# Delta-rule attention in front of two MLPs: state and solved rows as block-diagonal tiles, more fillers at the head of TensorE's queue, weight conversion in three passes

## The chip, the core and the metric

The kernel runs on one core of a Trainium2 chip. The metric is the device time of one execution in microseconds (us), the lower the better. Several executions are timed, and the median counts. One further execution was profiled: the times of single instructions below come from that one.

The engines are TensorE (PE; PEld is its weight load, which runs beside PE), VectorE (DVE), ScalarE (ACT), GpSimd (POOL) and SyncE (SP, which here only issues DMAs). Each works through its own queue in the order in which the program filled it.

## The reference

Three layers follow each other. First comes an attention with a state that is corrected at each position (the delta rule), 4 batches x 8 heads, 768 positions, 48 values per head:

```python
k_n = k / (np.linalg.norm(k, axis=-1, keepdims=True) + 1e-06)
for t in range(S):
    y[:, :, t] = einsum('bhd,bhde->bhe', q[:, :, t], state)
    v_old = einsum('bhde,bhd->bhe', state, k_n[:, :, t])
    state += beta[t] * einsum('bhd,bhe->bhde', k_n[:, :, t], v[:, :, t] - v_old)
```

Its output, 3072 tokens x 384, goes through two MLPs of width 2048: `g(x @ w_in) @ w_out` with a rational function g, and then the same with `h * tanh(softplus(h))`. The weights reach the core as 64-bit floats; the kernel makes two 32-bit parts of each (high and low), and every MLP product is three products of such parts.

## The kernel before

**Stages.** The attention comes first, on all engines at once, together with the conversion of the first MLP's weights. The two MLPs follow, 192 units of 9 up and 9 down products each; the second MLP's weights are converted beside the first MLP.

**Attention.** The 768 positions are cut into 12 blocks `u` of 64. A tile holds 16 pairs of heads, one head of a pair on the partitions 0 to 63, the other on 64 to 127. For each block there are three pieces of work:

- `prepare(u)`: load k and q (SP), square and sum k (ACT L315, DVE L319), invert the norm for two blocks at a time (DVE L329 to L344, ACT L333), scale k (L396, DVE for the first two blocks, POOL for the others), transpose k and q on PE (L352), copy them out of PSUM (ACT L356), multiply k with k and q (`gram`, PE L367), mask the result (DVE L376), copy blocks (ACT L414).
- `inverse(u)`, once for two blocks: invert a triangular 32 x 32 matrix for each head by 30 dependent steps (L451 and L457), between two 32 x 32 transposes on DVE (L439 `first`, L464 `last`, which writes `xt`) and two scalings by beta (L442, L461). `ON_DVE` puts the ones of blocks 1 and 9 on DVE; those of blocks 3, 5, 7 and 11 run on POOL.
- `step(u)`, in two halves `h`: keys with the state (`ks`, PE L511), subtract from v (`rest`, DVE L519), solve the upper 32 rows (`uu`, PE L528), copy out (`u_out`, ACT L535), `cross` (PE L543), `rest`, `uu` for the lower rows, `u_out`; then the new state (`s_mm`, PE L551; `s_out`, ACT L559) and the output (`y_mm`, two parts for each half, PE L566; `y_out`, ACT L575). Every product here is 64 x 64 or 32 x 32. Two products of different heads lie on opposite corners of the array.

A block can only be prepared when the block six before it is through its step (rings of `NT = 6`), a step needs the `xt` of its pair of blocks, and the state runs from step to step.

**Order.** All attention and conversion work is put into a `Plan` with a cost in ns for each piece. `Plan.best` plays 800 random priority changes through these costs with a greedy list order, keeps the best, and writes the engines' queues in that order. `HOP` is the cost of a handover between engines. Where the plan sees TensorE idle, `run` puts fillers (`heat`, L1060: products with a zero tile) into PE's queue, and 16 of them stand ahead of everything. They read `zero`, which POOL fills at the end of its setup (L1056), and `ident`.

**Conversion.** For each of 32 halves of w1: DMA, `mag` (ACT L669), `size` (DVE, two instructions, L674 and L678), `sign` (DVE L684), `low` (DVE L690), `out` (ACT L697), `rest` (POOL L702), and a DMA back to memory for each whole tile.

**Start of the MLP.** `fetch_x` loads the first rows of the attention's output, `x_hi` (ACT L802) and `x_lo` (POOL L806) split them into the tile `x`.

## Time and profile before

| | us |
|---|---|
| median of 3 runs | 1112.09 (1107.67 to 1112.23) |
| the profiled execution, its own time | 1106.31 |
| its span, first to last instruction | 1104.6 |
| PE busy in the span | 1052.0 (95%) |
| DVE, ACT, POOL busy | 722.8, 605.3, 545.7 |

The busy share of PE says little about the attention: fillers count as busy there, and pipelined products overlap. In the MLPs, from 310 us on, PE streams without a gap. The page's line of the granted clock shows full speed (9 in tenths) nearly throughout, with slices at 8 in the attention. The groups below are cut from the page's views for single stretches; an instruction's row has its start, its length, the engine, the line, what it writes and reads, its shape and how many follow each other as one row, and in brackets how long the engine had been idle and what ended that.

### The profile page before, as it was taken

Reading aid. Unit: us, or ns where it says so; the run is one execution under the profiler, and the core shown is the slowest. Engines: PE = TensorE matmul, PEld = TensorE weight load, DVE = VectorE, ACT = ScalarE, POOL = GpSimd, SP = SyncE. Lnnn points to the kernel's source line nnn. Section 1 sums busy time; section 2 is a strip of 40 time slices with the busy share of each in tenths; the row PEclk is TensorE's granted clock in tenths of the full one; section 3 lists DMA queues with packets and bytes.
Section 4 is the critical chain, followed back from the end, with each engine's and each line's share of the span. In section 5 each row is a group of like instructions: output and inputs, shape, how many; then the busy total and the mean of one; then the engine's idle time right before and its main releaser. Section 6 shows DMA issues by size and latency. Waiting matters only on the chain.

```text
span 1104.6 us, 24807 instructions
## 1 busy us (share of the span) xinstructions
PE 1052.0 (95%) x10128; PEld 898.2 (81%) x10128; DVE 722.8 (65%) x1221; ACT 605.3 (55%) x1081; POOL 545.7 (49%) x623
## 2 busy tenths in 40 slices
PE   5998999888899999999999999999999999999998
PEld 4887888777878878888888888888888888888897
DVE  5997574997669999999999999993222212222211
ACT  3515455433479888988989898743232322223222
POOL 3288797575458778787877878773000000000000
PEclk9999899998999999999999999999999999999999
DMA  6617776425775021121203036250110202011010
GB/s 127 150 30 182 184 202 161 130 61 156 221 263 223 15 101 44 53 76 63 96 10 106 15 127 252 74 177 1 24 34 13 46 1 57 1 23 35 10 20 30
DMA packets 152947, 99.25 MB, mean 90 GB/s; under 512 B 114048, under 2 KB 136192, under 8 KB 152832
## 3 DMA queue, kind: packets, MB, share of 16 engines
q1 hardware_dynamic: 150976, 96.77, 30.4%
q8 instruction: 79, 1.29, 0.5%
q10 hardware_dynamic: 1600, 0.79, 0.3%
q14 instruction: 36, 0.29, 0.1%
q0 software_dynamic: 256, 0.10, 0.1%
HBM read 66.16 MB, written 31.46 MB: 88 GB/s over the span
## 4 chain that ended last, share of the span: by engine, by line
PE 71%; DVE 15%; issue 3%; ACT 3%; DMA 3%; POOL 2%; SPq 2%; DVEq 0%; ACTq 0%; POOLq 0%
PE h L822 31%; PE o L848 28%; PE o L862 3%; PE c_ps L528 2%; PE y_ps L566 2%; DVE tmp L451 2%; PE c_ps L511 1%; SPq L240 1%; PE s_all L551 1%; DVE q L920 1%; DVE r L924 1%; DVE s L911 1%; DVE g L929 1%; DVE xs L457 1%; DMA w<-in_moe_w_in_dram 1%
## 5 line engine op out<-in xcount | busy, mean ns | idle before, releaser
L822 PE MATMUL h<-x,w 128*128 128x512 f32 x1728 | 424.3, 390 | 2.9 <-DVE s L913 2.9
L848 PE MATMUL o<-gh,w 128*128 128x512 f32 x1584 | 387.6, 389 | 0.0
L822 PEld LDWEIGHTS h<-x,w 128*128 128x128 f32 x1728 | 323.3, 188 | 72.3 <-DVE s L913 5.8
L848 PEld LDWEIGHTS o<-gh,w 128*128 128x128 f32 x1584 | 297.3, 188 | 61.8
L837 DVE TENSOR_TENSOR gh<-g,gh 128x512 fp32r<-128x512 f32 x80 | 55.0, 687 | 231.4 <-ACT g L949 231.4
L944 ACT ACTIVATE gh<-h 128x512 fp32r<-128x512 f32 x96 | 57.5, 599 | 261.0 <-PE h L822 261.0
L837 POOL TENSOR_TENSOR gh<-g,gh 128x512 fp32r<-128x512 f32 x112 | 149.5, 1336 | 83.5 <-ACT gh L833 62.0
L897 POOL TENSOR_TENSOR q<-q,r 128x512 f32<-128x512 f32 x96 | 126.0, 1313 | 24.4 <-ACT r L891 19.5
L893 ACT ACTIVATE s<-h,ab 128x512 f32<-128x512 f32 x96 | 74.0, 771 | 2.1 <-PE h L822 2.1
L702 POOL TENSOR_TENSOR w<-wm,w 128x384 fp32r<-128x384 f32 x48 | 49.6, 1036 | 50.2 <-ACT w L697 50.2
L913 DVE SCALAR_TENSOR_TENSOR s<-s,ab,h 128x512 f32<-128x512 f32 x96 | 71.8, 748 | 3.4
L924 DVE SCALAR_TENSOR_TENSOR r<-s,ab,r 128x512 f32<-128x512 f32 x96 | 71.9, 749 | 0.0
L911 DVE TENSOR_TENSOR s<-s,h 128x512 f32<-128x512 f32 x96 | 65.2, 679 | 9.0 <-ACT q L884 7.7
L833 ACT CAST gh<-g 128x512 fp32r<-128x512 f32 x96 | 59.4, 619 | 16.5 <-DVE g L929 15.8
L929 DVE SCALAR_TENSOR_TENSOR g<-q,r 128x512 f32<-128x512 f32 x96 | 65.9, 687 | 3.3
L457 POOL TENSOR_TENSOR xs<-xs,tmp 128x30 f32<-128x30 f32 (+14 forms) x120 | 63.4, 528 | 9.4
L904 ACT ACTIVATE r<-q,cst 128x512 f32<-128x512 f32 x96 | 66.0, 688 | 1.9 <-POOL q L897 1.9
L920 DVE SCALAR_TENSOR_TENSOR q<-q,r 128x512 f32<-128x512 f32 x96 | 65.3, 680 | 1.2 <-ACT r L906 1.1
L884 ACT ACTIVATE q<-h 128x512 f32<-128x512 f32 x96 | 57.4, 598 | 15.2 <-PE h L822 14.5
L451 POOL TENSOR_TENSOR tmp<-xs 128x30 f32<-128x30 f32 (+14 forms) x120 | 58.8, 490 | 6.7
L906 ACT ACTIVATE r<-r 128x512 f32<-128x512 f32 x96 | 55.9, 582 | 3.0
L949 ACT ACTIVATE g<-h 128x512 f32<-128x512 f32 x96 | 57.0, 594 | 0.0
(126 smaller groups left out, 1332.4 us busy)
## 6 DMA issues: line engine op xcount, KB each, us to landing
w<-w SPq DMA_DIRECT2D x36, 768.0 KB, 6.6
w<-in_moe_w_in_dram SPq DMA_DIRECT2D x32, 384.0 KB, 3.6
w<-in_moe_w_out_dram SPq DMA_DIRECT2D x32, 384.0 KB, 3.6
xraw<-x SPq DMA_DIRECT2D x36, 256.0 KB, 3.7
w<-wt SPq DMA_DIRECT2D x8, 768.0 KB, 3.7
kn<-in_k_dram SPq DMA_DIRECT2D x48, 96.0 KB, 3.5
qn<-in_q_dram SPq DMA_DIRECT2D x48, 96.0 KB, 3.3
v<-in_v_dram SPq DMA_DIRECT2D x48, 96.0 KB, 3.4
```

The source lines that it names most:

```text
L451: eng.tensor_tensor(out=tv, in0=ls[:, j, j + 1:HC].unsqueeze(1).to_broadcast([128, j, n]), in1=xs[:, 0:j, j:j + 1].to_broadcast([128, j, n ...
L457: eng.tensor_tensor(out=xs[:, 0:j, j + 1:HC], in0=xs[:, 0:j, j + 1:HC], in1=tv, op=ALU.add)
L822: self.nc.tensor.matmul(out=self.st[i]["h"], lhsT=self.w.t[f][:, a, 0, k], rhs=self.x[g][:, b, k], start=(n == 0), stop=(n == 8),)
L837: (nc.gpsimd if engine == "P" else nc.vector).tensor_tensor(out=s["gh"][:, 1], in0=s["g"], in1=s["gh"][:, 0].bitcast(F32), op=ALU.subtract)
L848: self.nc.tensor.matmul(out=self.acc[g][d], lhsT=self.w.t[f][:, a, 1, d], rhs=self.st[i]["gh"][:, b], start=(first and n == 0), stop=(last ...
L893: nc.scalar.activation(out=s["s"], in_=s["h"], func=ACTF.Identity, scale=k["a3"], bias=k["a2"])
L897: nc.gpsimd.tensor_tensor(out=s["q"], in0=s["q"], in1=s["r"], op=ALU.mult)
L911: nc.vector.tensor_tensor(out=s["s"], in0=s["s"], in1=s["h"], op=ALU.mult)
L913: nc.vector.scalar_tensor_tensor(out=s["s"], in0=s["s"], scalar=k["a1"], in1=s["h"], op0=ALU.add, op1=ALU.mult)
L920: nc.vector.scalar_tensor_tensor(out=s["q"], in0=s["q"], scalar=1.0 + 1e-6, in1=s["r"], op0=ALU.add, op1=ALU.mult)
L924: nc.vector.scalar_tensor_tensor(out=s["r"], in0=s["s"], scalar=k["a0"], in1=s["r"], op0=ALU.add, op1=ALU.mult)
L929: nc.vector.scalar_tensor_tensor(out=s["g"], in0=s["q"], scalar=2.0, in1=s["r"], op0=ALU.subtract, op1=ALU.mult, reverse0=True)
```

## The change

- State (`su`) and solved rows (`ud`, new, `V` in `step`) get a block-diagonal form, with zeros off the diagonal. `ks` and `s_mm` then make one product over all 128 rows with 96 moving columns for two heads, in place of two with 48: half as many products. The output's part on `V` also runs over 128 rows, with as many products as before.
- The halves `h` of a step are now the front and the back half of the pairs, not the two heads of a pair. `ud` is written by two ACT copies per half (`u_out`, 64 partitions each), beside one copy for the upper rows (`u_half`); the new state takes two copies per half. The output's second part needs all four copies of `V`.
- `gram` walks the array's four corners in another order.
- `xs`, `beta` and `U` move into the MLP's tile `x` and `tmp` into the tile `xraw`: `x_hi` now also waits for the last readers of `xs` and `U`, `fetch_x` for those of `tmp`.
- `zero` is filled first of all on DVE, fillers read only `zero`, and 30 stand ahead of everything.
- `size` is one DVE instruction in place of two; `mag` multiplies by a power of two.
- `beta` is loaded by 16 DMAs from POOL's queue in place of 8, behind `make_identity`. The two `su` tiles are twice as large, and `ud` is cleared too.
- `HOP` and several planned costs have other values, so all queues are written in another order.

```diff
-    HOP = 60
+    HOP = 100
@@ Attention.__init__, setup
-        self.su = ring("su", 2, [128, 2, M // 2, D])
-        self.u = ring("u", 1, [128, M, D])
+        self.su = ring("su", 2, [128, M // 2, 2, 2, D])
+        self.ud, = ring("ud", 1, [128, 2, M // 2, 2, DP])
-        self.xs = ring("xs", 2, [128, HC, HC])
+        self.tmp = [flat[:, 2 * M * HC + 256 * i:2 * M * HC + 256 * i + 256] for i in range(2)]
+        self.xs = [spare_x[:, HC * HC * i:HC * HC * i + HC * HC].rearrange("p (a b) -> p a b", a=HC) for i in range(2)]
+        self.u = spare_x[:, 2 * HC * HC:2 * HC * HC + M * D].rearrange("p (c n d) -> p c n d", c=2, n=M // 2)
-        for n in range(8):
-            nc.gpsimd.dma_start(out=self.beta[16 * n:16 * n + 16], in_=self.bv[n])
         make_identity(nc, self.ident)
+        for n in range(16):
+            nc.gpsimd.dma_start(out=self.beta[8 * n:8 * n + 8], in_=self.bv[n])
-        for t in self.su:
+        for t in [*self.su, self.ud]:
             nc.gpsimd.memset(t, 0.0)
@@ inverse
-            cost = 3.9 * n + 560 if engine == "POOL" else 2.1 * n + 300 if early else 2.8 * n + 240
+            cost = 3.7 * n + 480 if engine == "POOL" else 2.1 * n + 340 if early else 4.2 * n + 300
@@ step
         def ks(h):
+                for n in range(N * h, N * h + N):
+                    for a in range(2):
+                        rows = slice(64 * a, 64 * a + 64)
+                        nc.tensor.matmul(
+                            out=bank(h, rows)[:, :, n - N * h], lhsT=kq[:, 0, n, rows],
+                            rhs=S[:, n, a], start=True, stop=True,
+                        )
+        def u_half(h):
+            return lambda: nc.scalar.copy(out=U[:, :, N * h:N * h + N], in_=bank(h))
+        def u_out(h, a):
+            rows = slice(64 * a, 64 * a + 64)
+            return lambda: nc.scalar.copy(out=V[rows, :, N * h:N * h + N, a, 0:D], in_=bank(h, rows))
         def s_mm(h):
+                for n in range(N * h, N * h + N):
+                    for c in range(2):
+                        nc.tensor.matmul(
+                            out=s_bank(h, c)[:, n - N * h], lhsT=kn[:, 2 * n + c, 0:D], rhs=V[:, c, n, :, 0:D],
+                            start=False, stop=True, skip_group_check=True,
+                        )
+        def s_out(h, c):
+            return lambda: nc.scalar.copy(out=T[64 * c:64 * c + D, N * h:N * h + N, :, c], in_=s_bank(h, c))
+        def y_mm(c, part):
+                        nc.tensor.matmul(
+                            out=y_ps[64 * a:64 * a + D, o], lhsT=V[:, c, n, a, 0:D] if part else S[r, n, a, c],
+                            rhs=gm[:, m, HC:] if part else kq[r, 1, n, rows],
...
+                [f"V{h}{a}" for h in range(2) for a in range(2)] + [f"{gmb}{2 * c}", f"{gmb}{2 * c + 1}"] if part
@@ Weights.convert
-                out=w["x"].bitcast(F32), in0=w["m"].bitcast(F32), scalar1=self.LEAST, scalar2=self.MOST,
-                op0=ALU.max, op1=ALU.min,
-            )
-            nc.vector.tensor_scalar(
-                out=w["x"], in0=w["x"], scalar1=3, scalar2=0x3FFFFFF8,
-                op0=ALU.logical_shift_left, op1=ALU.bitwise_and,
+                out=w["x"], in0=w["m"], scalar1=3, scalar2=None, op0=ALU.logical_shift_left
@@ the kernel's body
+        nc.vector.memset(zero, 0.0)
         at.setup()
-        nc.gpsimd.memset(zero, 0.0)
-                out=at.s_ps[1][:, DM:DM + 128] if used else at.y_ps[:, 0:128], lhsT=zero, rhs=at.ident,
+                out=at.s_ps[1][:, DM:DM + 128] if used else at.y_ps[:, 0:128], lhsT=zero, rhs=zero,
-            plan.add("ACT", 620, lambda n=n: m1.x_hi(0, n), ["xr"], [f"x{n}"], early=late)
+            plan.add("ACT", 620, lambda n=n: m1.x_hi(0, n), ["xr"], [f"x{n}", "xs0", "xs1", "U0", "U1"], early=late)
-        for _ in range(16):
+        for _ in range(30):
             heat()
```

## Rows read from the trace of the kernel before

**Rows 1.** Windows: stretch, us, busy us (instructions) by engine, granted clock, DMA.

```profile
20.40:76.50 56.10, 51.78 (x596) 47.84 (x592) 50.35 (x127) 20.91 (x39) 23.89 (x38) 1.00 0.40 93
254.60:289.40 34.80, 31.11 (x912) 29.62 (x912) 21.69 (x38) 13.75 (x29) 23.85 (x37) 0.81 0.67 191
310.20:1104.60 794.40, 786.93 (x3509) 654.40 (x3504) 497.54 (x751) 473.20 (x820) 348.67 (x294) 1.00 0.22 69
```

**Rows 2.** Chain that ended last, in order of time: start us, us, what.

```profile
74.51 2.00 DVE xt L464
...
155.48 1.99 DVE xt L464
...
285.69 2.06 DVE xt L464
```

**Rows 3.** Waits of POOL, 53 to 282.2 us: total us, times, longest.

```profile
POOL w L702 <- ACT w L697: 20.5, 8, 6.0
```

**Rows 4.** Timeline of POOL: the longest of these waits.

```profile
255.55 1.00 POOL L702 TENSOR_TENSOR w<-wm,w 128x384 fp32r<-128x384 f32 x1 [6.05 <-ACT w L697]
```

**Rows 5.** Timeline of all engines, the head.

```profile
10.74 6.08 PE L1060 MATMUL y_ps<-ident,zero 128*128 128x128 f32 x32 [10.74 <-POOL zero L1056]
10.86 0.96 DVE L396 TENSOR_TENSOR kn<-kn,nrm 128x768 f32<-128x768 f32 x1
...
16.66 0.60 PE L352 MATMUL c_ps<-ident,kn 128*128 128x128 f32 x4
...
20.64 0.84 ACT L315 ACTIVATE gm<-kn 128x768 f32<-128x768 f32 x1
...
27.56 2.91 POOL L396 TENSOR_TENSOR kn<-kn,nrm 128x768 f32<-128x768 f32 x2 [16.87 <-DMA v<-in_v_dram]
```

**Rows 6.** Timeline of PE, fillers at full clock.

```profile
22.97 1.50 PE L1060 MATMUL y_ps<-ident,zero 128*128 128x128 f32 x12
```

**Rows 7.** Groups of DVE, 20 to 76.5 us, then 194.7 to 224: busy us, mean ns.

```profile
L678 DVE TENSOR_SCALAR word<-word 128x384 int32<-128x384 int32 x3 | 1.7, 566 | 0.1
...
L678 DVE TENSOR_SCALAR word<-word 128x384 int32<-128x384 int32 x2 | 1.1, 567 | 0.1
```

**Rows 8.** Timeline of PE: keys with state, then output.

```profile
264.91 1.14 PE L511 MATMUL c_ps<-su,kq 64*64 64x48 f32 x32 [0.58 <-ACT su L559]
...
265.88 1.06 PE L566 MATMUL y_ps<-gm,u 64*48 64x64 f32 x32
```

**Rows 9.** Timeline of PE: new state, 32 records.

```profile
101.75 0.92 PE L551 MATMUL s_all<-u,kn 64*48 64x48 f32 x32 [0.16 <-ACT u L535]
```

**Rows 10.** Timeline of PE: `gram`, two banks, all four corners.

```profile
27.15 0.28 PE L367 MATMUL t_ps<-kq 64*64 64x128 f32 x2
...
27.16 0.28 PE L367 MATMUL c_ps<-kq 64*64 64x128 f32 x2
```

**Rows 11.** Groups of ACT, 76.5 to 310 us: busy us, mean ns.

```profile
L535 ACT COPY u<-c_ps 128x384 f32<-128x384 f32 x48 | 22.8, 478 | 36.7 <-PE c_ps L528 36.0 <-DVE xs L457 0.6
...
L559 ACT COPY su<-s_all 128x384 f32<-128x384 f32 x22 | 10.4, 481 | 21.3 <-PE s_all L551 21.3
```

**Rows 12.** Timeline of PE: end of the attention.

```profile
306.12 1.10 PE L566 MATMUL y_ps<-gm,u 64*48 64x64 f32 x32
307.14 0.87 PE L528 MATMUL c_ps<-r,xt 32*32 32x48 f32 x32
307.94 1.10 PE L566 MATMUL y_ps<-kq,su 64*48 64x64 f32 x32
308.87 0.29 PE L566 MATMUL y_ps<-gm,u 64*48 64x64 f32 x3
...
310.24 4.37 PE L822 MATMUL h<-x,w 128*128 128x512 f32 x18
```

**Rows 13.** Timeline of ACT at that end.

```profile
307.26 0.59 ACT L575 COPY yst<-y_ps 128x512 f32<-128x512 f32 x1 [0.59 <-PE y_ps L566]
```

**Rows 14.** Timeline of POOL: the first low part of `x`.

```profile
282.10 1.28 POOL L806 TENSOR_TENSOR x<-xraw,x 128x512 fp32r<-128x512 f32 x1
```

More of the change, by code (lines that the diff above doesn't have):

```diff
@@ L469, in inverse @@
         if early:
-            p.add("ACT", 900, lambda: nc.scalar.copy(out=xs, in_=ls), lsb, xsb)
+            p.add("ACT", 1020, lambda: nc.scalar.copy(out=xs, in_=ls), lsb, xsb)
         p.add(engine, 150, diag, (), xsb)
@@ L508, in ks, with rest @@
         def ks(h):
             def f():
-                for n, a, r, rows in each(h):
+                for n in range(N * h, N * h + N):
+                    for a in range(2):
+                        rows = slice(64 * a, 64 * a + 64)
[3 more added lines that the diff above has]
+                        )
+            return f
+        def rest(h, src):
+            return lambda: nc.vector.tensor_tensor(
+                out=cols(r2, h), in0=cols(src, h), in1=bank(h), op=ALU.subtract,
+            )
@@ L525, in f, with cross @@
+        def cross(h):
             def f():
-                for n, a, r, rows in each(h):
-                    rows = slice(64 * a + HC * c, 64 * a + HC * c + HC)
+                for n, c, a, m in heads(h):
+                    src, dst = slice(64 * a, 64 * a + HC), slice(64 * a + HC, 64 * a + C)
                     nc.tensor.matmul(
-                        out=out(h, rows, n), lhsT=xt[rows, u % 2 * M + W * h + n, :], rhs=(r2 if u or c else v)[rows, W * h + n, :],
-                        start=True, stop=True,
-                    )
@@ new lines, in y_mm, with f @@
+        def y_mm(c, part):
+            def f():
+                for n in range(W):
+                    o, m = slice(n * C, n * C + C), W * c + n
+                    for a in range(2):
+                        rows, r = slice(64 * a, 64 * a + 64), slice(64 * c, 64 * c + 64)
+                        nc.tensor.matmul(
+                            out=y_ps[64 * a:64 * a + D, o], lhsT=V[:, c, n, a, 0:D] if part else S[r, n, a, c],
+                            rhs=gm[:, m, HC:] if part else kq[r, 1, n, rows],
+                            start=part == int(u == 0) and n == 0, stop=part > 0 and n == W - 1, skip_group_check=True,
+                        )
+            return f
@@ L573, in y_out, with y_add @@
-        def y_out(h):
-            o = yst.rearrange("p (h n) t -> p h n t", h=2)
-            return lambda: nc.scalar.copy(
-                out=o[:, h, :, g * C:(g + 1) * C], in_=y_ps.rearrange("p (n t) -> p n t", n=W)
-            )
-        def y_add(h, part):
-            need = [f"{ub}{h}", f"{gmb}{2 * h}", f"{gmb}{2 * h + 1}"] if part else [f"{sb}{h}", f"{kqb}1{0}", f"{kqb}1{1}"]
+        def y_add(c, part):
+            need = (
+                [f"V{h}{a}" for h in range(2) for a in range(2)] + [f"{gmb}{2 * c}", f"{gmb}{2 * c + 1}"] if part
+                else [f"{sb}{h}{c}" for h in range(2)] + [f"{kqb}10", f"{kqb}11"]
+            )
@@ L597, in step @@
-            p.add("ACT", 480, u_out(h), [c], [uh])
+                p.add("PE", 800, ks(h), [f"{kqb}0{h}", f"{sb}{h}0", f"{sb}{h}1"], [b])
+                p.add("DVE", 560, rest(h, v), [b, vb], [r])
+            p.add("PE", 950, uu(h, 0), [r if u else vb, xb], [b])
+            p.add("ACT", 480, u_half(h), [b], [uh])
+            p.add("PE", 950, cross(h), [f"{gmb}{h}", f"{gmb}{2 + h}", uh], [b])
+            p.add("DVE", 560, rest(h, r2 if u else v), [b] if u else [b, vb], [r])
+            p.add("PE", 950, uu(h, 1), [r, xb, "y_ps"] if h else [r, xb], [b])
@@ L598, in step @@
+            for a in range(2):
+                p.add("ACT", 480, u_out(h, a), [b], [f"V{h}{a}"])
         if u + 1 < self.NU:
             for h in range(2):
-                p.add("PE", 860, s_mm(h), [f"{ub}{h}", knb], [f"s_ps{h}"])
-                p.add("ACT", 480, s_out(h), [f"s_ps{h}"], [f"{tb}{h}"])
-        for h in (1, 0):
-            if not h:
+                p.add("PE", 800, s_mm(h), [f"V{h}0", f"V{h}1", knb], [f"s_ps{h}"])
+                for c in range(2):
+                    p.add("ACT", 480, s_out(h, c), [f"s_ps{h}"], [f"{tb}{h}{c}"])
```

154 lines of the change are left out of this document (62 added, 92 removed).

## The prediction

> **What bounds the kernel now.** I read the windows first. From 310.2 us to the end PE is busy 786.93 of 794.40 us at a granted clock of 1.00 [rows 1]: the MLPs run at TensorE's pace. The change takes a DVE pass out of the second MLP's conversion too, but DVE is no limit there, so I price this part at nothing; the cover is PE's own stream, and the 7.5 us in which PE is not busy are all that could come back. What is decided lies in the first 310 us.
>
> There the chain of waits runs over the transposes that deliver `xt`, the inverse of two blocks: the first, second and last of five rows end at 76.5, 157.5 and 287.7 us [rows 2]. After the first, steps 0 and 1 can run, after the last steps 10 and 11, which end with the attention at 310.24 [rows 12]. So the attention is a head of 76.5 us, a middle of 211 us set by inverses (mostly on POOL) and by steps that free their buffers, and a tail of 22.5 us. In the head from 20.4 us on DVE is busy 50.35 of 56.10 us [rows 1]: DVE is its bound. In the middle POOL waits eight times, 20.5 us in all, for ACT's part of a weight conversion queued ahead of its inverse [rows 3]; the longest wait, 6.05 us [rows 4], lies inside the last inverse, which leads straight to the last `xt`.
>
> **The head.** The 16 fillers wait for POOL's `zero` until 10.74, run to 16.82, and PE transposes the first keys only at 16.66, though DVE had scaled them by 10.86 + 0.96 = 11.82 [rows 5]. After the change DVE fills `zero` first, so the fillers can start near 1.7 us. There are 60 records in place of 32: 6.08 us for the first 32, as before, and 28 more at 1.50 / 12 = 0.125 us [rows 5, 6], 3.5 us, so to about 11.3. PE is then free before the keys: first transpose at 11.9, 4.7 us earlier. If the clock rose late, 60 records at the mean of the first 32 (0.19) take 11.4 us, to 13.1: 3.5 us earlier. What is late next are the keys of blocks 2 and 3: a DMA brings them whatever PE does, their last square ends on ACT at 21.48, and POOL scales them only at 27.56 [rows 5]. In the 6.1 us between, DVE works through the masks of block 0's products before it gets to their norm; these masks move forward with PE, the square does not. Bounds 0 and -4.7; I take **-3.5**, since DVE's queue and not the DMA fills most of the 6.1.
>
> POOL's setup, which now ends with `zero` by 10.74, gets 8 more DMAs to issue and larger memsets. Even twice as long it ends by 21.5, and POOL's first work comes at 27.56 [rows 5], or some 4 us earlier then: that gap is the cover, and I price this at 0. Without it each us of setup would be one of the inverse of block 3. DVE's masks are written before the large memsets, so they move less than the whole.
>
> `size` loses one of two instructions, 0.566 us; three sides are converted in the head [rows 7] and DVE is the bound there: **-1.7** (bound 0, if the plan puts other sides there). `mag` stays one ACT instruction.
>
> **The middle, conversion.** POOL's eight waits end on a chain through DVE. The shorter chain takes 0.57 us off each wait that DVE ended and nothing off one that a DMA ended: between 0 and -4.5; I take six of eight, **-3.4**. Two more sides lie between 194.7 and 224 us on DVE [rows 7], where it masks the Gram products of blocks 10 and 11 for the last inverse: **-1.1**, bound 0.
>
> **The middle, order.** The plan's costs change, and with them all queues. The DVE inverse of block 9 was planned at 2.8 n + 240 ns per step and is now at 4.2 n + 300; with n = j (31 - j) over 30 steps, 4960 in all, that is 21 and 30 us; where POOL waited 6.05 us, the conversion's DVE part had been put behind that inverse [rows 4]. With a dearer inverse the plan can place it ahead. I take half, **-3.0**, with bounds of -6.05 and +6.05: a reshuffled order can as well make a wait of that size anew.
>
> **The middle, PE.** A step's `ks` takes 264.91 to 265.88, 0.97 us per half, for 32 records [rows 8]; `s_mm` 0.92 [rows 9]. A record of 128 moving columns over the whole array takes 0.111 us, from twelve in 1.50 us less about the 0.28 that a product lasts [rows 6, 10], so 96 columns take 0.083. The new `ks` and `s_mm` have 16 records over 128 rows and half of the columns. If the two column halves run side by side, that is 8 x 0.083 = 0.67 us plus about 0.2 until the last result; if not, 1.33 plus 0.2. No row shows a 128-row product on half of the columns. The nearest are the `gram` rows: two records into one bank and two into the other start within 0.01 us [rows 10], four corners at once, so also two corners over the same rows. I take side by side. `ks` then gains 0.97 - 0.67 = 0.3 per half, to the next product, `s_mm` some 0.05: 0.7 per step. Against it stand new switches of the tile's shape, since `ks`, `s_mm` and the output's second part are now 128-row and its first part is not: an output pass takes 1.02 us before a 32 x 32 product (306.12 to 307.14) and 0.93 before another output pass (307.94 to 308.87) [rows 12], so 0.09 per switch, up to four more per step. Net -0.3 per step; on the six steps from block 6 on, **-1.8**. Bounds: -4.2 without switches; the upper end is the first rival.
>
> Fillers are 128-row products too, and with a weight load of 128 columns each they follow at 0.111 us, the time of their moving columns alone [rows 6]: load and product overlap on the same rows. [...]
>
> **The middle, ACT.** Copies out of PSUM: one more per half after the solve, one more per half for the state. Each lasts 0.48 us [rows 11]; 24 + 22 more make 22 us of ACT. Idle time of 36.7 us before the copies of `u` alone [rows 11] gives the room; but of the four more per step two are new links of the chain from solve to next solve, 0.96 us, hidden where PE has an output pass to do meanwhile. On the six late steps that is 0 to +5.8; I take half, **+2.9**.
>
> **The tail.** Before, half 1 finished first, and its output pass ran at 306.12 while half 0 was still solved; after the last solve (307.14 + 0.87 = 308.0) only two passes were left, one not waiting, to 310.24: 2.2 us [rows 12]. Now both output passes on `V` need all four copies. After the last solve: two copies (about 1.1 with handovers), a pass (0.93), the copy out of `y_ps` (0.59 [rows 13] and two handovers), two passes (1.9): 4.6 us. About 2.4 later, less what the shorter `ks` gives: **+2.0** (bounds 0 and +2.4). `x_hi` now waits for the last `cross`; then three ACT copies and three POOL subtractions of 1.28 us [rows 14], about 5 us, run beside these passes and the first three up products, which need only the high part: 0, and +1 if ACT's queue is late.
>
> **Sum:** -3.5 - 1.7 - 3.4 - 1.1 - 3.0 - 1.8 + 2.9 + 2.0 = -9.6 us. The profiled execution took 1106.31 us, so it becomes 1096.7; the median of the runs is 5.8 higher, 1112.09, and that difference is kept: **1102.5 us**.
>
> **Rivals.**
> 1. Column halves one after the other (slower). Per step `ks` costs 2 x (1.33 - 0.97) = +0.7, `s_mm` 2 x (1.33 - 0.72) = +1.2 (its 0.92 less 0.2 until the last result), the output's two 128-row passes, 32 records of 64 columns at 0.056 against 0.93, 2 x 0.86 = +1.7: 3.6 per step in place of the -1.8 in all. On six to eleven steps 22 to 40 us beside the sum's other terms: 1126 to 1144. It decides from a loss of some 2 us per step on, where it outweighs the rest of the sum. For it: no row shows such a product. Against: [rows 10]. Chance 0.08.
> 2. Load and product of a 128-row tile in turn (slower). With loads at the same pace per column, 64 columns of `ks` add 0.056 to 0.083 for each pair of records, 48 of `s_mm` 0.042, 48 of the output 0.042 to 0.056: 8 x 0.139 = 1.11, 8 x 0.125 = 1.00, 16 x 0.098 = 1.57 us, so 2 x (0.14 + 0.28 + 0.64) = 2.1 per step, on six to eleven steps 13 to 23 us: 1117 to 1127. Against it stand the fillers' 0.111 us per record with loads as wide as the product [rows 6]. Chance 0.03. [...]
> 3. ACT takes the place: the two copies lengthen all twelve steps, 11.5 us for 2.9, and PE idles meanwhile. [...] 1102.5 + 8.6 + 3.3 = 1114. Chance 0.10; with a new POOL wait as large as [rows 4] (+9.05 against the sum) 1123, chance 0.07.
> 4. The gates hold their times (the loads, POOL's inverses), and the conversions' gain goes into idle time: head and tail alone leave some -3, 1109. Chance 0.11.
> 5. A better fit of the plan: of POOL's 20.5 us [rows 3] the sum took 6.4; the other 14 gone too give 1088. Chance 0.11.
>
> **How the numbers follow.** My forecast has 0.50; its own bounds run from 1093 to 1112. The range reaches over cases 3 and 4 above and into case 5 below: **1084 to 1119**. Left out are case 1, most of case 2, the 1123 of case 3 and the bottom of case 5, about 0.19. A measurement of this kernel can tell about 0.5%, 5.6 us, from no change. Faster by more: 0.47 of the forecast, case 5, 0.03 of case 4: 0.61. Within it: the forecast's upper end, most of case 4, the 1114 of case 3: 0.21. Slower: cases 1 and 2 and the 1123: 0.18.
>
> **What would show it.** First transpose near 12 us in place of 16.66; first `xt` at 71 to 72; a `ks` half of 16 records in about 0.67 us from first to next product (1.33 would be rival 1, 1.1 rival 2); fewer and shorter waits of POOL for ACT; last `xt` near 276; from the last solve to the first up product 4.6 us in place of 2.2. The prediction is wrong if the attention's end stays at 310 or the MLPs' 794 us move.

## The result, and the profile after

The changed kernel took 1121.03 us (median of 20 executions, 1108.28 to 1128.61), the kernel before, beside it, 1108.64 (1100.07 to 1118.38). The ratio is 1.0065 with an interval of 1.0042 to 1.0089; it leaves out the five executions that lay more than 1.5% above the fastest, so it is smaller than the ratio of the medians. Forecast were 1102.5 us: the sign was wrong. The profiled execution took 1115.84 us (span 1114.1) for 1106.31 before.

First windows, each with stretch, us, busy us (instructions) of PE, PEld, DVE, ACT and POOL, granted clock, DMA share and GB/s. Before: the 30 steps of DVE's inverse of block 9, then from the fifth `xt` (blocks 8 and 9) to the first up product, then steps 10 and 11 alone.

```profile
208.90:250.90 42.00, 34.01 (x1009) 30.72 (x1008) 40.16 (x84) 14.94 (x28) 23.87 (x40) 0.96 0.21 60
254.50:310.20 55.70, 51.25 (x1646) 48.27 (x1646) 33.91 (x61) 24.39 (x51) 29.95 (x42) 0.88 0.64 192
...
289.39:310.24 20.85, 20.17 (x737) 18.65 (x736) 12.12 (x22) 10.64 (x22) 6.11 (x6) 1.00 0.61 192
```

The same three stretches after, and the MLPs, which answer to the last of [rows 1].

```profile
198.30:251.30 53.00, 45.54 (x994) 40.65 (x993) 45.74 (x89) 19.25 (x37) 27.98 (x48) 0.87 0.18 42
...
255.10:322.00 66.90, 60.58 (x1456) 55.61 (x1456) 32.20 (x57) 35.02 (x72) 31.41 (x44) 0.72 0.58 183
...
285.96:322.02 36.06, 32.73 (x716) 29.76 (x716) 15.62 (x29) 17.82 (x37) 11.30 (x11) 0.67 0.54 168
...
322.00:1114.10 792.10, 785.81 (x3508) 655.06 (x3504) 478.47 (x719) 470.87 (x820) 353.72 (x295) 1.00 0.22 69
```

Then PE's timeline, after: start, us, instruction, in brackets the idle time before it and what ended it. It answers to [rows 5, 8, 12].

```profile
11.37 0.63 PE L354 MATMUL t_ps<-ident,kn 128*128 128x128 f32 x4 [1.06 <-issue]
...
72.76 1.55 PE L534 MATMUL c_ps<-v,xt 32*32 32x48 f32 x64 [0.64 <-DVE xt L466]
...
211.92 0.87 PE L534 MATMUL c_ps<-r,xt 32*32 32x48 f32 x32 [1.16 <-DVE xt L466]
...
255.14 2.53 PE L534 MATMUL c_ps<-r,xt 32*32 32x48 f32 x58 [3.30 <-DVE xt L466]
...
282.88 1.10 PE L579 MATMUL y_ps<-kq,su 64*48 64x64 f32 x32 [1.77 <-ACT yst L588]
283.90 0.88 PE L519 MATMUL c_ps<-su,kq 128*64 128x96 f32 x16
284.61 1.06 PE L579 MATMUL y_ps<-gm,ud 128*48 128x64 f32 x32
285.96 1.55 PE L534 MATMUL c_ps<-r,xt 32*32 32x48 f32 x64 [0.28 <-DVE xt L466]
...
292.67 0.62 PE L579 MATMUL y_ps<-gm,ud 128*48 128x64 f32 x16
295.13 0.32 PE L579 MATMUL y_ps<-gm,ud 128*48 128x64 f32 x2 [1.84 <-ACT ud L545]
...
313.91 1.49 PE L534 MATMUL c_ps<-r,xt 32*32 32x48 f32 x32
315.33 2.08 PE L1070 MATMUL s_all<-zero 128*128 128x128 f32 x8
317.33 1.95 PE L579 MATMUL y_ps<-gm,ud 128*48 128x64 f32 x32
...
320.99 1.10 PE L579 MATMUL y_ps<-gm,ud 128*48 128x64 f32 x32
322.02 1.20 PE L832 MATMUL h<-x,w 128*128 128x512 f32 x4
```

And rows of before's PE: the first products of steps 6, 8 and 10, the last with the fillers ahead of it.

```profile
215.50 0.87 PE L528 MATMUL c_ps<-r,xt 32*32 32x48 f32 x32 [1.22 <-DVE xt L464]
...
254.59 2.53 PE L528 MATMUL c_ps<-r,xt 32*32 32x48 f32 x58 [4.14 <-DVE xt L464]
...
286.61 1.10 PE L566 MATMUL y_ps<-kq,su 64*48 64x64 f32 x32 [0.69 <-ACT yst L575]
287.63 1.83 PE L1060 MATMUL s_all<-ident,zero 128*128 128x128 f32 x14
289.39 1.55 PE L528 MATMUL c_ps<-r,xt 32*32 32x48 f32 x64
```

**What the reader is to see.** The attention ends 11.78 us later (322.02 for 310.24), and it loses this time in one place. Step 8 starts at 255.14 in place of 254.59: the whole gain of head, conversion and order has come to +0.55. Steps 8 and 9 take 30.82 us in place of 34.80, 4.0 less (1.8 us of the 34.80 are the fillers ahead of step 10). Steps 10 and 11 take 36.06 in place of 20.85, 15.2 more. In the last 66.9 us the granted clock is 0.72, before it was 0.88 over 55.7. In windows of 1 us both traces show two levels, 1.00 and 0.50, and values between them only where one gives way to the other (after, 1.00 from 268 to 295 us and 0.50 from 296 to 319; before, 0.50 from 255 to 264 and 1.00 from 265 to 281). At the lower of the two that is 2 x 0.28 x 66.9 = 37 us, before 13 us. PE did not wait for the last `xt` before: that ended at 287.75 [rows 2], when PE's real work ahead of step 10 ended too (286.61 + 1.10), and fillers filled the 1.7 us to step 10. The `xt` that PE waited for was the fifth, 4.14 us before and 3.30 after.

Over the whole span the mean granted clock was 0.962 after and 0.984 before; 2 x (1 - clock) x span gives 85 and 35 us at the lower level, which the texts below call half clock. These are the profiled executions; in the median of all executions it is 98 us for the changed kernel and 35 to 39 for the runs of before in each group.

### The profile page after: what moved, and what is told of

Same layout as the page of the kernel before. It is cut to its first block, busy times and chain, and to the rows that moved or that the text cites. A ratio compares the mean times of both kernels' runs of the same rounds, so it can differ in the third digit from the quotient of the medians.

```text
span 1114.1 us, 23271 instructions
## 1 busy us (share of the span) xinstructions
PE 1063.7 (95%) x9376; PEld 905.5 (81%) x9376; DVE 694.9 (62%) x1158; ACT 626.9 (56%) x1127; POOL 557.3 (50%) x631
## 4 chain that ended last, share of the span: by engine, by line
PE 72%; DMA 2%; ACT 1%; DVE 0%; issue 0%; POOL 0%; SPq 0%; ACTq 0%; DVEq 0%
PE h L832 35%; PE o L858 32%; PE o L872 3%; PE y_ps L579 1%; DMA x<-yst 1%; DMA w<-in_moe_w_in_dram 1%; PE c_ps L534 0%; PE c_ps L551 0%; PE c_ps L519 0%; PE s_all L1070 0%; DMA out_dram<-ev 0%; PE s_all L564 0%; POOL q L907 0%; ACT ev L1046 0%; ACT w L707 0%
## 5 line engine op out<-in xcount | busy, mean ns | idle before, releaser
L847 POOL TENSOR_TENSOR gh<-g,gh 128x512 fp32r<-128x512 f32 x112 | 146.7, 1311 | 70.5 <-ACT gh L843 48.7
L907 POOL TENSOR_TENSOR q<-q,r 128x512 f32<-128x512 f32 x96 | 131.0, 1365 | 28.1 <-ACT r L901 23.2
L459 POOL TENSOR_TENSOR x<-x,xraw 128x30 f32<-128x30 f32 (+14 forms) x120 | 63.2, 527 | 9.4
L453 POOL TENSOR_TENSOR xraw<-x 128x30 f32<-128x30 f32 (+14 forms) x120 | 58.3, 486 | 7.2
```

Of the source, the lines that this page charges most:

```text
L459: eng.tensor_tensor(out=xs[:, 0:j, j + 1:HC], in0=xs[:, 0:j, j + 1:HC], in1=tv, op=ALU.add)
L847: (nc.gpsimd if engine == "P" else nc.vector).tensor_tensor(out=s["gh"][:, 1], in0=s["g"], in1=s["gh"][:, 0].bitcast(F32), op=ALU.subtract)
L907: nc.gpsimd.tensor_tensor(out=s["q"], in0=s["q"], in1=s["r"], op=ALU.mult)
```

## The experiments

Three theories stood against each other. C: TensorE's granted clock makes the loss, and the block form makes the clock fall. A: the added ACT copies lengthen the chain of each step. O: the order of the queues makes it, which the plan draws anew with every edit.

"Kept" means that the work other than the edit stands in the old order in all queues; "drawn" that the plan wrote a new one. The half-clock time is that of the profiled execution, then the median of all. Each group had runs of the kernel before beside it, with medians of 1107.87 to 1108.86.

| kernel | order | us, median | ratio to before, interval | us at half clock, profiled / median |
|---|---|---|---|---|
| before with conversion and fillers | drawn | 1111.16 | 1.0036 (1.0009 to 1.0064) | 69 / 58 |
| the same | kept | 1109.01 | 0.9989 (0.9958 to 1.0020) | 64 / 58 |
| before with split copies | drawn | 1119.34 | 1.0107 (1.0066 to 1.0148) | 81 / 68 |
| the same | kept | 1112.25 | 1.0031 (1.0006 to 1.0056) | 42 / 29 |
| changed, old conversion and fillers | drawn | 1119.48 | 1.0100 (1.0060 to 1.0141) | 85 / 79 |
| changed, `ks` twice | kept | 1125.26 | 1.0155 (1.0104 to 1.0207) | 95 / 80 |
| changed, denser fillers | kept | 1139.67 | 1.0286 (1.0231 to 1.0341) | 94 / 71 |
| before, denser fillers | kept | 1132.51 | 1.0201 (1.0147 to 1.0254) | 29 / 25 |
| changed, fillers in one gap | kept | 1119.75 | 1.0100 (1.0061 to 1.0138) | 89 / 89 |
| changed, no planned fillers | kept | 1123.22 | 1.0111 (1.0072 to 1.0150) | 161 / 167 |
| before, seed 1 | drawn | 1114.83 | 1.0064 (1.0033 to 1.0095) | 54 / 50 |
| before, seed 2 | drawn | 1120.51 | 1.0096 (1.0066 to 1.0126) | 52 / 51 |
| before, changed planned costs | drawn | 1120.46 | 1.0100 (1.0056 to 1.0144) | 31 / 59 |
| changed, seed 1 | drawn | 1108.59 | 1.0009 (0.9974 to 1.0043) | 100 / 83 |
| changed, seed 2 | drawn | 1113.45 | 1.0030 (1.0005 to 1.0055) | 78 / 78 |
| changed, copies on ACT and DVE, seed 0 | drawn | 1114.70 | 1.0046 (1.0022 to 1.0070) | 89 / 91 |
| the same, seed 1 | drawn | 1114.50 | 1.0062 (1.0034 to 1.0090) | 62 / 68 |
| the same, seed 2 | drawn | 1116.21 | 1.0065 (1.0029 to 1.0100) | 81 / 71 |

### The parts alone

**Conversion and fillers**, put into the kernel before, first with a new order:

```diff
+        nc.vector.memset(zero, 0.0)
         at.setup()
-        for _ in range(16):
+        for _ in range(30):
@@ Weights.convert: mag, size and sign as in the changed kernel
-                p.add("DVE", 1160, size, [m], ["word"], early=late)
+                p.add("DVE", 560, size, [m], ["word"], early=late)
```

> The kernel before with the three-pass conversion and the fillers first (zero on DVE, 30 of them, reading only zero); its attention products, state tiles, copies, HOP and planned costs stay. Theory C (what is lost in the changed kernel is lost by the block form, through TensorE's granted clock): this part alone keeps its gains, first transpose of the keys at 11 to 12 us, first xt at 72 to 73, half-clock stretches in the attention no longer than before's 34 us in sum, time 4 to 8 us below the kernel before. Theory O (the loss comes from the queues' new order, which any edit of the conversion throws anew): first transpose at 11 to 12, but later xt anywhere, time within 10 us of the kernel before on either side. Theory A (the loss is the added ACT copies): as C.

First transpose at 11.8 us, but first `xt` at 77.2 and 1111.16 us. Theories C and A, which had a gain, are missed; theory O had left 10 us open on either side. The same with the old planned costs, so that the order is kept:

```diff
-                p.add("DVE", 560, size, [m], ["word"], early=late)
+                p.add("DVE", 1160, size, [m], ["word"], early=late)
-                p.add("DVE", 570, sign, [m], ["word"], early=late)
+                p.add("DVE", 570, sign, [raw], ["word"], early=late)
```

> The kernel before with the three-pass conversion and the fillers first, with the planned costs and needs of the old conversion, so that all queues keep the order of before but for the setup. Theory O (the 1111 of the earlier kernel with the same edits came from its new order): 3 to 8 us below the kernel before, first transpose at 11 to 12, half-clock stretches 25 to 45 us. Theory C, in the form that these two edits themselves idle TensorE: 1109 to 1113, half-clock stretches 55 to 80 us.

1109.01 for 1108.86: nothing, with an interval of -4.7 to +2.2 us. That is theory C's form (64 us at half clock, 58 in the median for 38 in the runs of before beside it), not O's. These are the parts to which the sum gave -9.7. Where they went is seen in this kernel's timelines of ACT (the squares of blocks 2 and 3), DVE, POOL and PE, and in POOL's waits (total us, times, longest) from 53 to 285 us:

```profile
19.19 0.84 ACT L315 ACTIVATE gm<-kn 128x768 f32<-128x768 f32 x1 [3.17 <-DMA kn<-in_k_dram]
...
21.61 0.84 ACT L315 ACTIVATE gm<-kn 128x768 f32<-128x768 f32 x1 [1.10 <-DMA kn<-in_k_dram]
```

```profile
20.06 0.95 DVE L319 TENSOR_REDUCE nrm<-gm 128x16 f32<-128x768 f32 x1 [4.44 <-ACT gm L315]
20.93 0.55 DVE L376 TENSOR_TENSOR gm<-t_ps,mask 128x384 f32<-128x384 f32 x1
```

```profile
27.80 2.91 POOL L396 TENSOR_TENSOR kn<-kn,nrm 128x768 f32<-128x768 f32 x2 [17.33 <-ACT kq L356]
```

```profile
78.44 0.87 PE L528 MATMUL c_ps<-v,xt 32*32 32x48 f32 x32 [0.61 <-DVE xt L464]
```

```profile
POOL w L694 <- ACT w L689: 18.4, 7, 5.8
```

The squares wait for the keys' DMA and run at 19.19 and 21.61; before, the last of them stood at 20.64 behind copies [rows 5], and there it looked like a matter of ACT's queue. DVE idled 4.44 us for the first of them, because its sum stands ahead of block 0's masks in DVE's queue, so the masks did not move forward with PE. POOL scales at 27.80, before at 27.56. The first `xt` ends 1.9 us later than before (78.4 for 76.5); the rest of this delay was not traced. POOL's waits are 18.4 us with a longest of 5.8, before 20.5 and 6.0 [rows 3]: 2.1 us less, and the last `xt` came at 291.2, not earlier than before's 287.7.

**Split copies**, put into the kernel before, with a new order and then as one piece of the plan at the old cost:

```diff
-            p.add("ACT", 480, u_out(h), [c], [uh])
+            for a in range(2):
+                p.add("ACT", 480, u_part(h, a), [c], [uh])
@@ and s_out likewise; in the second kernel both copies in one p.add
```

> The kernel before with the copies of the lower solved rows and of the new state each cut into two ACT copies of 64 partitions, as the changed kernel has them; nothing else. Theory A (added copies lengthen the chain of each step by 0.5 us twice, and idle TensorE): 6 to 12 us above the kernel before, the stretch from last xt to first up product 26 to 30 us against 22.5. Theory C in the form that TensorE's waits let the clock fall: the same, and half-clock stretches of over 60 us against 34. Theory C in the form that the missing records let it fall: 0 to 4 us above, half-clock stretches 25 to 45 us.

> The kernel before with the lower solved rows and the new state copied by two ACT copies of 64 partitions each, the two issued as one piece of the plan at the old planned cost, so that all queues keep the order of before. Theory A (the copies lengthen the chain of the steps): 4 to 12 us above the kernel before. Theory O (the 1119 of the earlier kernel with split copies came from its new order): within 3 us of the kernel before.

1119.34 drawn, 1112.25 kept. The copies as such cost 3.4 us (0.7 to 6.2), between the two expectations; some eight of the 11.5 us of the first kernel go with its order.

**Block form without the conversion and the fillers:** the changed kernel with the `Weights` class, the 16 fillers and the setup order of before.

```diff
-        nc.vector.memset(zero, 0.0)
         at.setup()
+        nc.gpsimd.memset(zero, 0.0)
-        for _ in range(30):
+        for _ in range(16):
```

> The changed kernel with the conversion, the fillers and the setup order of before; block-diagonal state and solved rows, split copies, HOP 100 and the new planned costs stay. Theory C: 10 to 16 us above the kernel before, half-clock stretches of 70 to 100 us in the attention against 34, the stretch from the last xt to the first up product 32 to 37 us against 22.5. Theory A: 5 to 12 us above, that stretch 26 to 30 us at a clock no lower than before's 0.81. Theory O: time on either side, no fixed length of that stretch.

1119.48 and 85 us at half clock, as theory C had it, but last `xt` to first up product was 28.5 us, as A had it. Both theories' times include 1119.48. It decides nothing, as later runs show that a draw of the order is worth as much.

### The clock

**`ks` twice:**

```diff
         def ks(h):
             def f():
+                for _ in range(2):
```

> The changed kernel with every product of keys with state issued twice, the second time with the same result: 16 records more per half, so TensorE gets back the number of records that the block form took from it there. Theory C, in the form that missing PE work lets the clock fall: half-clock stretches of the attention fall from 85 us to 50 or less, and the time stays within 3 us of the changed kernel or falls up to 8 below it, although each step from the third on has 1.3 us more on its chain. Theory A, and C in the form that PE's waits and not its record count let the clock fall: half-clock stretches stay at 75 to 100 us, time 6 to 15 us above the changed kernel.

95 us at half clock, 80 in the median of six executions for 98 in the changed kernel, far from the 50 of theory C: the records that the block form saves in `ks` are at most a small part of it. 4.2 us more, under the 6 of the other theories.

**Denser fillers, and none:**

```diff
-    WINDOW, IDLE = 3400, 600
+    WINDOW, IDLE = 3400, 0
-        plan.run(heat, 200)
+        plan.run(heat, 125)
@@ the kernel without planned fillers
-                    n = max(0, int((t - last - max(0, self.IDLE - gone)) * 0.9 // unit))
+                    n = 0 * max(0, int((t - last - max(0, self.IDLE - gone)) * 0.9 // unit))
```

> The changed kernel with more fillers: the planned idle of TensorE is filled from its first ns on (IDLE 0 in place of 600), one filler for each 125 ns of it in place of 200. The other work stands in the same order on every engine. Theory C (the loss is TensorE's granted clock, which falls after stretches in which TensorE idles): half-clock stretches of the attention fall from 85 to below 50 us, the time falls by 8 to 20 us, to 1101 to 1113. Theory O (the queues' order makes the loss, the clock only goes with it): half-clock stretches may fall, but the time stays within 4 us of the changed kernel or grows with the fillers' own time.

> The kernel before with the same denser fillers, its other work in its own order. Theory C: before has only 34 us at half clock, so no more than 0 to 8 us are to be had here; if the block form shortens the work and only the clock hides it, this kernel stays above the changed kernel with the same fillers. Theory O: within 3 us of the kernel before or above it.

> The changed kernel without the fillers that the plan puts between the products of the attention (the 30 at the head stay, and the 12 in the last step go too); the queues keep their order. It measures what the clock is worth against what fillers cost. Theory C (an us at half clock costs nearly half an us): half-clock stretches grow to 150 us or more and the time to 1135 or above. Rival (the attention hangs on DVE, POOL and ACT, and fillers delay real products, as denser fillers cost 19 us): half-clock stretches grow, but the time stays within 8 us of the changed kernel on either side.

Theory C fails as a remedy. Denser fillers cost 18.6 us in the changed kernel and 24 us in the kernel before, although the half-clock time went down in both (medians 98 to 71 and 35 to 25 us). Without planned fillers it grows from 98 to 167 us, and the time by 2.2 us (four executions), which is the rival's case: as far as these runs show, fillers cost about as much as the clock that they buy.

**Fillers in one gap**, that at 293.3 to 295.1 us of the changed kernel:

```diff
@@ y_mm
+                    if part and c == 1 and u == self.NU - 2 and n == N - 1:
+                        for _ in range(14):
+                            self.drain(True)
```

> The changed kernel with 14 fillers at one place more: in step 10, in the middle of the first output pass on V, where TensorE idled for 1.84 us waiting for ACT's copies before its clock fell for 23.9 us. All queues keep their order. Theory C (the fall follows that idle stretch and costs the tail 12 us; fillers there cost nothing, since TensorE waits anyway): the tail stays at full clock, last xt to first up product 23 to 27 us in place of 36, the executions near 1122 vanish and the median comes to 1108 to 1113. Theory O or A (the tail is long by its copies, and the clock is an accompaniment): the tail stays at 32 us or more, median 1119 to 1123.

The clock stayed up behind the gap (0.98 from the last `xt` on), as theory C had it, and last `xt` to first up product was 29.2 us for 36.1; the median moved by 1.3 us only, as O and A had it. The profiled execution shows why that proves little: it lost elsewhere. Up to 303 us this kernel's instructions are those of the changed one, and so the two executions can be laid side by side. PE of the changed kernel at its step 6, with the window:

```profile
220.92 0.87 PE L564 MATMUL s_all<-ud,kn 128*48 128x96 f32 x16
```

```profile
215.20:232.30 17.10, 15.16 (x434) 13.46 (x434) 14.90 (x31) 10.06 (x19) 3.00 (x5) 1.00 0.02 5
```

and of the kernel with fillers in the gap, with the window, the fillers and the window of its tail:

```profile
213.28 0.87 PE L534 MATMUL c_ps<-r,xt 32*32 32x48 f32 x32 [1.74 <-DVE xt L466]
...
227.46 1.52 PE L564 MATMUL s_all<-ud,kn 128*48 128x96 f32 x16
...
304.04 3.39 PE L1073 MATMUL s_all<-zero 128*128 128x128 f32 x28
```

```profile
215.20:232.30 17.10, 17.10 (x288) 15.40 (x288) 8.50 (x22) 7.47 (x14) 0.00 (x0) 0.50 0.01 2
...
295.70:324.90 29.20, 27.68 (x768) 25.10 (x764) 15.44 (x29) 17.76 (x37) 10.70 (x10) 0.98 0.66 200
```

From the first product of step 6 to its first new state: 9.00 us (211.92 to 220.92) at full clock, 14.18 (213.28 to 227.46) where the clock fell. One execution came out of an idle time of 1.16 us with its clock, the other came out of 1.74 us and lost it for 17.1 us. So time at half clock does cost, 5.2 us here, where PE was busy throughout. What differs ahead of the fall is half an us of waiting. That this decided it is not shown, and the length of one wait does not decide alone: the changed kernel came out of 1.77 us at 282.88 at full clock. The fillers themselves took 3.39 us in a gap of 1.84: 14 fillers are 28 records. The remedy paid some 1.5 us for what it gained.

### The order

**Other seeds** for the plan's 800 trials: the same instructions, another order.

```diff
-        kinds, rng = sorted(set(self.kinds)), random.Random(0)
+        kinds, rng = sorted(set(self.kinds)), random.Random(1)
```

> The kernel before with another seed for the 800 trials of its plan: the same instructions in another order of the queues. Theory O, in the form that the kernel before has a lucky order and any edit draws a new one: 1113 to 1122 and half-clock stretches of 60 to 90 us, as the conversion, the split copies and the block form each had when put in alone. Theory C in the form that each edit itself makes TensorE idle: within 4 us of the kernel before, half-clock stretches of 25 to 45 us.

> The changed kernel with another seed for the 800 trials of its plan: the same instructions in another order. Theory O: anywhere between 1100 and 1128, with half-clock stretches and the stretch from last xt to first up product far from the changed kernel's 85 and 36 us. Theory C in the form that the block form itself makes TensorE idle: within 5 us of the changed kernel, half-clock stretches of 70 to 100 us.

> The kernel before with a third seed for its plan's trials. Theory O (the order of before is better than most that the plan draws): 1111 to 1122. Rival (seed 1 was an unlucky draw, and before's order is a usual one): 1105 to 1110.

> The changed kernel with a third seed. Theory O (its order draws anywhere in a band as wide as that of before, and the change itself moves the middle of the band little): 1105 to 1124, the mean of the three seeds of the changed kernel within 4 us of the mean of the three of before. Rival (the block form itself costs, by its copies and the clock): 1115 or more, and the mean of three over 4 us above that of before.

Theory O has both kernels' seeds, but for the half-clock time of before's seed 1 (54 us for its 60 to 90). Three orders of before: 1108.6, 1114.8, 1120.5, mean 1114.6. Three of the changed kernel: 1121.0, 1108.6, 1113.5, mean 1114.4. As ratios the means are 1.0053 and 1.0035. The bands lie on each other; before's order is the best of its three, the changed kernel's the worst of its three. Three draws with a spread of 6 us each give the difference of the means a standard error of 5 us (6 x the root of 2/3), so a gain or a loss of several us by the change itself, up to some 10, is not excluded.

**The planned costs alone**, in the kernel before:

```diff
-    HOP = 60
+    HOP = 100
-            cost = 3.9 * n + 560 if engine == "POOL" else 2.1 * n + 300 if early else 2.8 * n + 240
+            cost = 3.7 * n + 480 if engine == "POOL" else 2.1 * n + 340 if early else 4.2 * n + 300
```

> The kernel before with HOP 100 and the changed kernel's planned costs of the inverses, nothing else: the same instructions in the order that these costs give. The prediction's step (a dearer inverse lets the plan put the conversion ahead of it, worth 3.0 us at the wait of 6.05): 1103 to 1107 and no wait of POOL over 4 us right after DVE's inverse of block 9. Theory O (another draw from the band): 1110 to 1122, with that wait or another of its size.

The median is theory O's. The profiled execution, the fastest of ten (1113.07 us), shows POOL's conversions behind the DVE inverse of block 9, the window from the fifth `xt` on, and step 10's first product:

```profile
260.96 0.99 POOL L702 TENSOR_TENSOR w<-wm,w 128x384 fp32r<-128x384 f32 x1 [0.74 <-ACT w L697]
...
263.77 1.00 POOL L702 TENSOR_TENSOR w<-wm,w 128x384 fp32r<-128x384 f32 x1 [0.77 <-ACT w L697]
```

```profile
259.90:317.00 57.10, 52.30 (x1632) 49.23 (x1632) 33.95 (x61) 24.61 (x51) 23.00 (x31) 0.82 0.59 176
```

```profile
289.89 0.87 PE L528 MATMUL c_ps<-r,xt 32*32 32x48 f32 x32 [0.18 <-DVE r L519]
```

The wait of 6.05 us at this place [rows 4] is down to 0.74, just as the step had it, and the last `xt` ends at 281.0 us, 6.7 earlier than before. The attention ends at 317.0, 6.8 later. Step 10 begins at 289.89, 9 us after its `xt`, on the result of DVE's subtraction: it waits for the state from step 9. What set the end was the fifth `xt`, at 259.9 for 254.5, and the four steps behind it.

**The second copy on DVE**, so that the two run side by side, under three seeds:

```diff
-                p.add("ACT", 480, u_out(h, a), [b], [f"V{h}{a}"])
+                p.add("DVE" if a else "ACT", 480, u_out(h, a), [b], [f"V{h}{a}"])
@@ s_out likewise
```

> The changed kernel with the second copy of each pair (solved rows, new state) on DVE in place of ACT, so that the two run side by side; the plan knows it and draws another order. Theory A (the serial second copy lengthens the chain of the steps): 4 to 12 us below the changed kernel's 1121, the last xt to the first up product 24 to 30 us. Theory O: anywhere from 1105 to 1125. Rival (DVE, which masks and runs an inverse, becomes later by 46 copies of 0.5 us): 1121 to 1130.

> The changed kernel with the copies side by side on ACT and DVE, and the second seed, under which the changed kernel took 1108.6. Theory A (the copies side by side are worth the 6 us of the first seed): 1100 to 1105, under both kernels. Theory O (the 6 us were a draw): 1105 to 1122.

> The same with the third seed, under which the changed kernel took 1113.5. Theory A: 1105 to 1110. Theory O: 1105 to 1122, the mean of the three seeds within 3 us of the 1114.4 of the changed kernel's three.

The first seed fits theory A (6.3 us less, last `xt` to first up product 29.9 us), but the other two took 5.9 and 2.8 us more than the changed kernel under the same seed: 1114.7, 1114.5 and 1116.2, mean 1115.1 beside 1114.4. The 6.3 us were a draw. No kernel tried was clearly faster than the kernel before.

## Why the prediction was wrong

**The step that failed first: "after the last steps 10 and 11".** The prediction let the last `xt` set the end, and summed into it whatever took POOL or the conversion forward. Before, PE began step 10 at 289.39, 1.7 us after that `xt`, without waiting for it. The chain of waits [rows 2] does run through that `xt`, but it goes on from there in DVE's queue to a weight conversion, not to step 10:

```profile
285.69 2.06 DVE xt L464
287.74 0.47 DVE word L684
```

The gate is the fifth `xt`: PE waits 2.0 to 6.7 us for it in 17 of the 20 kernels on record, 4.14 and 3.30 in these two. (With denser fillers in the changed kernel it waits 0.21 us, under seed 2 of before and with copies on ACT and DVE under seed 1 not at all: a gate, too, belongs to an order.) Behind it stand four steps whose state runs from one to the next, 55.7 us before, 57.0 with the changed costs. So the order's -3.0 was worth nothing at this place, or at most the 1.7 us of the fillers, whatever POOL did; the kernel with the changed costs has the earlier `xt` and ends later. The sum's last `xt` was to come near 276; it came at 285.9.

**The middle: DVE's inverse.** The fifth `xt` comes from DVE's inverse of block 9. Before, DVE is busy 40.16 of the 42.0 us that its steps take. After, they begin 10.6 us earlier (198.3 for 208.9) and end at the same time: 53.0 us, of which 45.74 busy. So 5.6 us more of busy time lie inside and 5.4 us more of idle time. Of the idle time 3.62 us are one wait:

```profile
241.52 0.55 DVE L526 TENSOR_TENSOR r<-v,c_ps 128x384 f32<-128x384 f32 x1 [3.62 <-PE c_ps L519]
```

```profile
239.87 1.55 PE L519 MATMUL c_ps<-su,kq 128*64 128x96 f32 x16
```

A subtraction of step 7 stands in DVE's queue ahead of the inverse's last seven steps, and it waits for a `ks` half that PE ran at half clock (1.55 us for its 16 records, 0.88 at full clock). There the head's gain came to an end; at step 6's first product it was still 3.6 us (211.92 for 215.50). The rival "the gates hold their times" had the mechanism, though not this gate.

**The head: right to the first transpose, wrong behind it.** 11.37 us, forecast about 12. In the kept order nothing of it reached the first `xt`, outside the bounds 0 and -4.7 even: the keys of blocks 2 and 3 arrive by DMA, and "these masks move forward with PE" was the mis-read step, since the sum of block 2's squares stands ahead of them in DVE's queue. The changed kernel's first `xt` at 72.7 (forecast 71 to 72) goes with its new order; in the kept one it came at 78.4.

**The conversion:** -1.7, -3.4 and -1.1 together with the head's -3.5 were -9.7; the kept order gives -1.2 (-4.7 to +2.2). Only where nothing was claimed did it pay: the MLPs took 792.1 us for 794.4, and 792.5 in both kernels that have the conversion without the block form, while the block form with the old conversion had 794.0. "I price this part at nothing" was wrong by 2.3 us; PE's idle time there went from 7.5 to 6.3 us.

**PE's products: right in size.** A `ks` half of 16 records takes 0.71 us to the next product (283.90 to 284.61), forecast 0.67, where rival 1 had 1.33 and rival 2 1.11. That is the pace of column halves side by side. The half's 16 weight loads, over the same 128 rows as its products, took 0.69 us from 283.90 on, in the same stretch: load and product overlap here. Rivals 1 and 2 fall. What this is worth per step was not measured by itself.

**POOL's longer setup and the first split of `x`: right.** Both were priced at nothing, and neither reached the path. POOL's setup ended at 18.2 us, and its first scaling began at 26.21, for 27.56 before [rows 5]; ACT and POOL had split the first rows of `x` by 313.3, and the first up product at 322.02 followed the last output pass without a wait.

**ACT's copies: right in size.** +2.9 in the forecast, +3.4 (0.7 to 6.2) for split copies alone, in the kept order of before.

**The tail and the clock: right in form, and the second step that failed.** From the last solve to the first up product 4.6 us were forecast. Under seed 1 PE's timeline has, from the last solve on,

```profile
314.56 0.87 PE L534 MATMUL c_ps<-r,xt 32*32 32x48 f32 x32
...
320.29 1.89 PE L832 MATMUL h<-x,w 128*128 128x512 f32 x7
```

which is 4.9 us (315.43 to 320.29), fillers included. In the changed kernel itself it is 6.6 us (315.40 to 322.02), most of it at half clock. The forecast's +2.0 for the tail stands against +15.2 for steps 10 and 11. In them PE idled 3.3 us for 0.7 before, and was busy 12.6 us longer with fewer records (716 for 737). At 0.67 over 36.06 us, 23.8 us ran at the lower level, before none. The same output pass of 32 records took 1.95 us there (317.33) and 1.10 at full clock (320.99), so this clock cost some 10 us, an estimate. In the kernel with fillers in the gap, whose tail kept its clock, the same two steps took 28.0 us, 8.0 less, with some 1.5 of the fillers' own. For the clock the sum had no term at all; it stood only in rival 3, at 3.3 us. No run shows these 3.3 us; what the runs showed in their place are the some 10 us here, an estimate, and the 5.2 us at step 6 of the kernel with fillers in the gap.

**The order as such** had bounds of plus and minus 6.05, the size of one wait. The three orders of before differ by 11.9 us and the three of the changed kernel by 12.4. The loss of 12.4 us between the medians is as large as what separates a good draw from a bad one; the runs do not show that the change itself costs anything, and not that it gains.

**What stays open.** In the median of its executions the changed form ran at half clock for 68 to 98 us under every order tried, the kernel before with its own products for 35 to 59. Why is not settled: giving `ks` its records back left 80 us, and the conversion with the fillers raised it too (58 in both orders). Nor is it settled what this clock costs in all: between the twenty executions of the changed kernel the time goes with the clock (1108.28 us at a mean of 0.965, 1128.61 at 0.950; a straight line through them has 0.48 us for each us at half clock), but a late wait can make both, the changed kernel under seed 1 had 83 us at half clock and took 1108.59, and without planned fillers 69 us more at half clock went with 2.2 us. What steps 10 and 11 would take in an unchanged order was not tried, since the block form's pieces of work have no place in before's order.

## What to carry to other kernels

Where a plan is drawn anew by every edit, measure how far draws of the same instructions lie apart before a gain of a few us is believed or forecast, and price each part in a kept order. Before time is summed into a gate, look at the row of who waits for it: a result that its reader takes up 1.7 us later, behind fillers, is no gate, even where the chain of waits runs through it. Denser fillers lowered the time at half clock in both kernels here (medians 98 to 71 and 35 to 25 us), and cost more than they gave (18.6 and 24 us more in all).

## What was not expected of the hardware

The clock fell to 0.50 behind idle times of PE of only 1.74 us (at 213.28, one gap filled) and 1.84 us (at 295.13, the changed kernel); behind 1.77 us (at 282.88, the changed kernel) it stayed at 1.00. It stayed at 0.50 for the 17.1 us and some 24 us that followed, although PE was busy in 17.10 of the 17.10 us of the first. In the second case it rose after 8 records of fillers (from 315.33 on) and an output pass, in the first without fillers. And the same instructions took 9.00 us in one execution and 14.18 us in another.
